# Attention with a gated MLP on one core: the last query tile's minimum taken by an accumulating tensor_scalar

## The chip, the cores and the metric

The kernel runs on one core of one Trainium2 chip. The metric is the device time of one execution in microseconds (us); of several executions the median is given.

## The reference

Block-causal attention over 8 batches x 8 heads with 576 positions of 64 dimensions, then a gated MLP over the 4608 tokens:

```python
scores = scale * np.matmul(q, k.transpose(0, 1, 3, 2))        # (8, 8, 576, 576)
mask = pos[:, None] // 64 >= pos[None, :] // 64
scores = np.where(mask, scores, -1e9)
attn = np.exp(scores - np.max(scores, axis=-1, keepdims=True))
attn = attn / (np.sum(attn, axis=-1, keepdims=True) + 1e-09)
x = np.matmul(attn, v)                                        # as (4608, 512)
h = x @ w_in                                                  # (4608, 2048)
g = h * erf(softplus(h))
return g @ w_out                                              # (4608, 512)
```

## The kernel before

The 64 heads go through attention one after the other, as a software pipeline over `n`, lines 515 to 556. In turn `n` the loop merges several lists of steps into one order: the loads of head n+3 (`load_qk`), the row maxima of head n+2 (`maxes`), the probabilities of head n (`probs`), the products with v of a pair of earlier heads (`pv`), and, after each four heads, the division by the sums (`normalise`). `merged` spreads each list evenly over the turn. Steps of the MLP for the first 6 of 16 chunks of d_ff (`moe1`, `moe_unit`, `gate`) fill the gaps of TensorE. After the last head the rest of these steps runs, and then the other 10 chunks for all tokens (lines 569 to 611).

The instructions that this order emits are put on the engines' queues by a scheduler: it goes by the emitted order, in which some kinds of steps are moved by a fixed number of instructions (`PRIO`, line 493: `pv` 74 ahead, weights 400 back or 300 ahead), and by when it takes operands and buffers to be ready. Each engine then runs its queue strictly in that order, and waits on semaphores where an operand comes from elsewhere.

The change is in `maxes(n)`. It computes the scores with queries on partitions (`mm`, L324: TensorE, into a bank of PSUM) and takes each row's maximum, negated, on VectorE (`red`, L327: a `tensor_reduce` with max and negate). The result is a column of `mx`, a [128, 6] tile in SBUF, one column for each of the five query tiles. The last query tile has 64 rows and 576 keys, more than a bank of PSUM holds, so its keys go in two halves of 288: step `d(0)` writes column 4, step `d(1)` column 5. Step `e` then takes the smaller of the two negated maxima with a one-column `tensor_tensor` (L352), transposes the first five columns on TensorE (L354, into `mt`), copies them on ScalarE (L356) and sends them by a DMA (L357) into the row of `qh` that `probs` uses two turns later.

Other lines that matter below. L312 and L313 are subtractions on GpSimd (POOL) for a head's load, L137 is GpSimd's subtraction in `gate`. L382 is VectorE's subtraction of the float16 part of the probabilities, L130 and L135 are VectorE's steps of `gate`, L469 its multiplication in `normalise`, L292 and L276 its work on v in `prep_v`. L370 and L371 are the score matmuls of `probs`; L414 and L437 are `pv`.

`bank` hands out PSUM: four buffers of one bank each in `ps_a` once the MLP runs beside attention. A score bank is free again when its reduction on VectorE has ended.

Of the kernel before, what the change touches and what calls it, by code (L numbers as in the profile page):

```python
# [15 lines left out]
AX = mybir.AxisListType  # L16
# the top word of the float64 2**-126, read as a float32
LEAST = 0.25 * (1 + 0.125) * 2.0**-13
PSUM = bass.MemoryType.PSUM

# erf(softplus(h)) as a function of r0 = tanh(T0 * h + T1).  Each step makes the next r:
#   ("S", i):    (p[0] * r_i + p[1]) ** 2
#   ("M", i, j): (r_i + p[0]) * r_j
#   ("A", i, j): p[0] * r_i + r_j
# and the value is the last r plus FIN.
PROG = [('S', 0), ('S', 1), ('M', 2, 2), ('M', 1, 3), ('M', 4, 4)]
# [8 lines left out]
def tile_attention_moe(ctx: ExitStack, tc: tile.TileContext, qk, v, w, maskrows, sels, out):  # L35
# [7 lines left out]
    F1 = 6  # L43
# [45 lines left out]
    def load_weight(whi, wlo, stage, f):  # L89
        """the two float32r parts of chunk f of both weights, out of the words of their float64"""  # L90
        for s in range(2):
            nm = f"{f}_{s}"
            raw = stage[0][0].tile([P, stage[0][2]], I32, tag=stage[0][1][s], bufs=stage[0][3], name=f"raw{nm}")[:, : 2 * DM].rearrange("p (n t) -> p n t", t=2)
            nc.sync.dma_start(raw.rearrange("p n t -> p (n t)"), w[f, s].bitcast(I32))
            top, low = raw[:, :, 1], raw[:, :, 0]
            # sign, exponent and 20 bits of mantissa as a float32 (0 for what is below its range)
            bits = stage[1][0].tile([P, stage[1][2]], I32, tag=stage[1][1], bufs=stage[1][3], name=f"bits{nm}")[:, :DM]
            nc.vector.tensor_scalar(out=bits, in0=top, scalar1=3, scalar2=0x3FFFFFF8, op0=ALU.logical_shift_left, op1=ALU.bitwise_and)  # L98
            nc.vector.scalar_tensor_tensor(out=bits, in0=top, scalar=-0x40000000, in1=bits, op0=ALU.bitwise_and, op1=ALU.bitwise_or)  # L99
            sq = stage[2][0].tile([P, stage[2][2]], F32, tag=stage[2][1], bufs=stage[2][3], name=f"sq{nm}")[:, :DM]  # L100
            nc.scalar.activation(sq, f32(top), AF.Square)
            nc.vector.scalar_tensor_tensor(out=sq, in0=sq, scalar=LEAST * LEAST, in1=f32(bits), op0=ALU.is_ge, op1=ALU.mult)  # L102
            # the low word, of the weight that the exponent gives it
            nc.vector.tensor_scalar(out=bits, in0=sq.bitcast(I32), scalar1=-0x800000, scalar2=None, op0=ALU.bitwise_and)  # L104
            nc.vector.scalar_tensor_tensor(out=f32(bits), in0=low.bitcast(U32), scalar=2.0**-52, in1=f32(bits), op0=ALU.mult, op1=ALU.mult)  # L105
            nc.scalar.copy(whi[:, s, :], sq)
            nc.gpsimd.tensor_tensor(out=sq, in0=sq, in1=f32(whi[:, s, :]), op=ALU.subtract)
            nc.gpsimd.tensor_tensor(out=wlo[:, s, :], in0=sq, in1=f32(bits), op=ALU.add)
        return whi, wlo
# [3 lines left out]
    def gate(h, name, gpool):  # L113
        """g = h * erf(softplus(h)) as a sum of two float32r parts"""
        n = h.shape[1]
        last = {}
        for k, o in enumerate(PROG):
            for i in o[1:]:
                last[i] = k
        gh, gl = (gpool.tile([P, n], F32R, tag=t, name=f"{name}_{t}") for t in ("gh", "gl"))  # L120
        regs = [mpool.tile([P, n], F32, tag="r0", name=f"{name}_r0")]
        free = [f32(gl), mpool.tile([P, n], F32, tag="r1", name=f"{name}_r1")]
        nc.scalar.activation(regs[0], h, AF.Tanh, bias=const(p1), scale=p0)  # L123
        for k, (o, pp) in enumerate(zip(PROG, pars)):
            free += [regs[i] for i in sorted(set(o[1:])) if last[i] == k]
            r = free.pop()
            if o[0] == "S":
                nc.scalar.activation(r, regs[o[1]], AF.Square, bias=const(pp[1]), scale=pp[0])  # L128
            elif o[0] == "M":
                nc.vector.scalar_tensor_tensor(out=r, in0=regs[o[1]], scalar=pp[0], in1=regs[o[2]], op0=ALU.add, op1=ALU.mult)  # L130
            else:
                nc.vector.scalar_tensor_tensor(out=r, in0=regs[o[1]], scalar=pp[0], in1=regs[o[2]], op0=ALU.mult, op1=ALU.add)
            regs.append(r)
        g = regs[-1]
        nc.vector.scalar_tensor_tensor(out=g, in0=g, scalar=fin, in1=h, op0=ALU.add, op1=ALU.mult)  # L135
        nc.scalar.copy(gh, g)  # L136
        nc.gpsimd.tensor_tensor(out=gl, in0=g, in1=f32(gh), op=ALU.subtract)  # L137
        return gh, gl
# [4 lines left out]
    def moe_unit(ws, xh, xl, o, tw, nu, u, name, first, last, spread):  # L143
        """nu chunks of d_ff over tw tokens: the steps to their g, and those to their part of o"""
        turns.append(u)
# [25 lines left out]
    def merged(*lists):  # L171
        """the steps of all lists, each list (steps, from, to) spread evenly over its part of the whole"""
        order = []
        for n, (steps, lo, hi) in enumerate(lists):
            order += [(lo + (hi - lo) * (i + 0.5) / len(steps), n, i) for i in range(len(steps))]
        return [lists[n][0][i] for _, n, i in sorted(order)]
# [4 lines left out]

# [1 line left out]
    def load_x(pool, t, tw):  # L183
# [33 lines left out]
    def moe1(ready, lag):  # L217
        """the next step of the first F1 chunks, if there is one: a unit up to its g together with an earlier unit from g on"""
        t = len(xs1)
# [19 lines left out]
    with tc.tile_pool(name="apool", bufs=2) as apool, tc.tile_pool(name="spool", bufs=1) as spool, \  # L239
# [4 lines left out]
        nc.sync.dma_start(sel, sels)  # L244
        # columns of the keys' tiles 0, 3, 4 and 1, 2 in the two parts of a head's probabilities
        p32s = [spool.tile([P, n], F32, name=f"p32_{i}") for i, n in enumerate(PN)]
# [10 lines left out]
        def bank(name):  # L257
            """a bank of PSUM; all of them take part as long as the other chunks of d_ff need none"""
            turn.append(0)
            k = len(turn) % 8 if not xs1 else 0  # L260
            if k in (2, 5):
                return ps_h.tile([P, 512], F32, tag="h", name=name)
            if k in (3,):
                return ps_o.tile([P, 512], F32, tag="o", name=name)
            return ps_a.tile([P, 512], F32, tag="a", name=name)
# [6 lines left out]
        def prep_v(b, qd, v32):  # L272
            """two float16 parts of v over its largest magnitude, and that magnitude"""
            nm = f"{b}_{qd}"
# [21 lines left out]
        def part(n, i):  # L296
            """part i of head n: kl over kh, qh over ql, kh over 5 rows that mask, qh over 5 rows that mask"""
            return qks[n % NB][:, i * S : (i + 1) * S]
# [18 lines left out]
        def maxes(n):  # L317
            """the steps to the rows' maxima, negated, in the row of t that goes with the ones"""
            mx, K = mxs[n % 2], D + 4
# [26 lines left out]
            def d(j):  # L346
                s = bank(f"s4_{n}_{j}")
                mm(s, 4, 288 * j, 288)
                red(4 + j, s[:64, :288], 64)

            def e():
                nc.vector.tensor_tensor(out=mx[:64, 4:5], in0=mx[:64, 4:5], in1=mx[:64, 5:6], op=ALU.min)  # L352
                pt = bank(f"mt{n}")
# [7 lines left out]
        def probs(n, out):  # L361
            """the steps to exp(0.125 * s - its maximum), keys on partitions, in two float16 parts"""
            K = D + 5
# [25 lines left out]
        def pv(qd, pp, prs, V, usb, rs):  # L389
            """the steps to the unnormalised outputs of heads 2pp and 2pp+1 of the quad, and to their sums"""  # L390
            vsb, vh, vl = V
            st = {}

            def ranges(q0, q1):
                """keys' tiles that a part of the queries attends to: the queries, and where their probabilities are"""
                for j in range(5):
# [21 lines left out]

            # the sums of two heads' first 384 and last 192 queries, in a group of 32 columns each
            order = []  # L420
# [24 lines left out]
        def normalise(b, qd, usbs, rs):  # L445
            nm = f"{b}_{qd}"
            # pair, tile of the sums, part of the queries, head
            ri = apool.tile([P, 2, 3, 2, 2], F32, tag="ri", name=f"ri{nm}")
# [36 lines left out]
        def late(kind, steps):  # L485
            """steps whose instructions the scheduler holds behind the next ones of the order, or ahead of some (offsets in instructions)"""
            def run(f):
# [69 lines left out]

# [1 line left out]
    N2 = 2  # L559
# [89 lines left out]
```

## Time and profile before

| | |
|---|---|
| median of 3 runs | 1399.85 us |
| the three runs | 1399.85, 1400.71, 1387.88 us |
| profiled execution | span 1407.0 us; its own time is not among the three |
| TensorE (PE) busy | 1273.8 us, 91% |
| VectorE (DVE) busy | 1013.9 us, 72% |
| ScalarE (ACT) busy | 793.2 us, 56% |
| GpSimd (POOL) busy | 602.1 us, 43% |

The profile is of one execution. PE are matmuls, PEld the loads of weights into TensorE, which overlap them. A share over the whole span mixes stages: attention with a part of the MLP fills about the first 735 us, the rest of the first six chunks and the preparation of weights the time to about 942 us, and the other chunks the end. An engine's idle time is put down to what ended it. In a line of a view that lists instructions, `mx<-s` means that the instruction writes the tile `mx` and reads the tile `s`, and `64x1 f32<-64x288 f32` gives partitions x elements of both.

### The profile page before, as it was taken

What the parts mean: (1) busy time and instruction counts of PE and PEld (TensorE: products, weight loads), DVE (VectorE), ACT (ScalarE), POOL (GpSimd) and SP (SyncE); (2) the same over time, 40 slices, a digit from 0 to 9 for tenths busy, and PEclk for the clock granted to TensorE, in tenths of its full rate; (3) what the DMA queues carried; (4) which work ended last, traced back from release to release, by engine and by line L of the source; (5) the groups of instructions that cost most, each with busy time, mean ns of one, the idle gap of its engine ahead of it and who ended that gap; (6) DMA issues with size and microseconds to landing.
All of it is one profiled execution on the core that took longest, in us unless ns stands there. A gap on an engine that the chain in (4) does not pass through costs nothing. (4 is left out here: it accounts for less than half of the span.)

```text
span 1407.0 us, 21952 instructions
## 1 busy us (share of the span) xinstructions
PE 1273.8 (91%) x8198; PEld 1026.1 (73%) x8198; DVE 1013.9 (72%) x1525; ACT 793.2 (56%) x1493; POOL 602.1 (43%) x454
## 2 busy tenths in 40 slices
PE   3798789989899898999889898779999999999998
PEld 1455567777777787777777787568888888888887
DVE  5768997788878788788697648996555555564654
ACT  1456566667666676667567455544444454445453
POOL 3757665445554554544445424562222222222221
PEclk9879899999999999999999899899999999999999
DMA  8557655757657576566623542302211311321110
GB/s 228 135 125 204 173 156 137 185 154 193 179 129 207 146 196 175 152 161 177 174 81 137 188 164 95 130 0 78 102 60 68 113 60 60 108 72 61 60 61 30
DMA packets 89370, 179.95 MB, mean 128 GB/s; under 512 B 8540, under 2 KB 27292, under 8 KB 89264
## 3 DMA queue, kind: packets, MB, share of 16 engines
q1 hardware_dynamic: 79280, 159.41, 38.1%
q0 software_dynamic: 9344, 18.97, 6.1%
q8 instruction: 65, 1.06, 0.3%
q10 hardware_dynamic: 640, 0.17, 0.1%
q14 instruction: 41, 0.34, 0.1%
HBM read 112.29 MB, written 37.75 MB: 107 GB/s over the span
## 5 line engine op out<-in xcount | busy, mean ns | idle before, releaser
L130 DVE SCALAR_TENSOR_TENSOR m_r<-m_r 128x512 f32<-128x512 f32 x288 | 232.9, 809 | 229.3 <-ACT m_r L128 225.8
L137 POOL TENSOR_TENSOR m_gl<-m_r,m_gh 128x512 fp32r<-128x512 f32 x144 | 195.5, 1357 | 443.7 <-ACT m_gh L136 359.2
L136 ACT CAST m_gh<-m_r 128x512 fp32r<-128x512 f32 x144 | 89.2, 619 | 251.9 <-DVE m_r L135 251.7
L154 PE MATMUL m_h<-xh,whi 128*128 128x256 f32 (+1 forms) x648 | 213.3, 329 | 17.3 <-DVE m_r L135 17.3
L128 ACT ACTIVATE m_r<-m_r,c 128x512 f32<-128x512 f32 x288 | 207.9, 722 | 11.0 <-ACT m_r L128 0.4
L154 PE MATMUL m_h<-xl,whi 128*128 128x256 f32 (+1 forms) x648 | 211.1, 326 | 0.3 <-DMA xl<-x_d 0.3
L154 PE MATMUL m_h<-xh,wlo 128*128 128x256 f32 (+1 forms) x648 | 211.1, 326 | 0.0
L327 DVE TENSOR_REDUCE mx<-s 64x1 f32<-64x288 f32 (+4 forms) x384 | 167.9, 468 | 56.4 <-PE s L324 53.9
L375 ACT ACTIVATE p<-t 128x288 f32<-128x288 f32 (+4 forms) x384 | 143.1, 388 | 97.9 <-PE t L371 76.2
L164 PE MATMUL o<-whi,m_gh 128*128 128x512 f32 x432 | 173.8, 403 | 6.7 <-ACT ob L209 4.3
L164 PE MATMUL o<-wlo,m_gh 128*128 128x512 f32 x432 | 173.8, 402 | 0.0
L382 DVE TENSOR_TENSOR pl<-p,ph 128x832 f16<-128x832 f32 (+1 forms) x128 | 158.5, 1240 | 18.0 <-ACT ph L381 17.8
L312 POOL TENSOR_TENSOR qk<-st,qk 64x576 fp32r<-64x576 f32 x64 | 103.2, 1613 | 157.5 <-PE s L324 55.9
L154 PEld LDWEIGHTS m_h<-xh,whi 128*128 128x128 f32 x648 | 126.6, 195 | 37.8 <-DVE m_r L135 21.9
L164 PE MATMUL o<-whi,m_gl 128*128 128x512 f32 x432 | 153.0, 402 | 0.2 <-POOL m_gl L137 0.2
L370 PE MATMUL t<-qk 69*128 69x288 f32 (+4 forms) x384 | 136.0, 355 | 12.6 <-DVE mx L327 7.0
L324 PE MATMUL s<-qk 68*128 68x256 f32 (+3 forms) x384 | 126.6, 362 | 14.3 <-DVE mx L327 8.7
L313 POOL TENSOR_TENSOR qk<-st,qk 64x576 fp32r<-64x576 f32 x64 | 111.3, 1739 | 65.5 <-DMA qk<-qk 61.7
L154 PEld LDWEIGHTS m_h<-xl,whi 128*128 128x128 f32 x648 | 126.5, 195 | 15.8 <-DMA xl<-x_d 0.6
L154 PEld LDWEIGHTS m_h<-xh,wlo 128*128 128x128 f32 x648 | 126.9, 196 | 9.4
L371 PE MATMUL t<-qk 128*128 128x288 f32 (+4 forms) x384 | 129.8, 339 | 0.0
L123 ACT ACTIVATE m_r<-m_h,c 128x512 f32<-128x512 f32 x144 | 98.8, 686 | 50.5 <-PE m_h L154 48.7
(84 smaller groups left out, 2499.1 us busy)
## 6 DMA issues: line engine op xcount, KB each, us to landing
st<-qk SPq DMA_DIRECT2D x64, 288.0 KB
qk<-qk POOLq DMA_DIRECT2D x64, 288.0 KB, 4.6
qk<-qk SPq DMA_DIRECT2D x64, 288.0 KB
x_d<-xs SPq DMA_DIRECT2D x32, 576.0 KB
raw<-w SPq DMA_DIRECT2D x32, 512.0 KB
v<-v SPq DMA_DIRECT2D x16, 640.0 KB
qk<-qk SPq DMA_DIRECT2D x64, 144.0 KB
xh<-x_d SPq DMA_DIRECT2D x18, 512.0 KB
```

The lines of the kernel that those rows point to most:

```text
L128: nc.scalar.activation(r, regs[o[1]], AF.Square, bias=const(pp[1]), scale=pp[0])
L130: nc.vector.scalar_tensor_tensor(out=r, in0=regs[o[1]], scalar=pp[0], in1=regs[o[2]], op0=ALU.add, op1=ALU.mult)
L137: nc.gpsimd.tensor_tensor(out=gl, in0=g, in1=f32(gh), op=ALU.subtract)
L154: nc.tensor.matmul(h[:, k, :], lhsT=a[:, 0, sl], rhs=x[:, cc, :], start=cc == 0 and i == 0, stop=cc == NCC - 1 and i == 2)
L164: nc.tensor.matmul(o[c], lhsT=a[:, sl], rhs=b_[:, 1, :], start=first and k == 0 and not lo and b_ is whi, stop=last and k == nu - 1 and lo)
L313: nc.gpsimd.tensor_tensor(out=t[D:, 1, :], in0=st[D:, :], in1=f32(t[D:, 1, :]), op=ALU.subtract)
L324: nc.tensor.matmul(dst[:r, :w_], lhsT=qh[:K, i * P : i * P + r], rhs=kh[:K, k0 : k0 + w_], start=True, stop=True)
L327: nc.vector.tensor_reduce(out=mx[:r, col : col + 1], in_=src, axis=AX.X, op=ALU.max, negate=True)
L370: nc.tensor.matmul(s[:kk, :w_], lhsT=kh[:K, ks], rhs=qh[:K, q0 : q0 + w_], start=True, stop=False)
L371: nc.tensor.matmul(s[:kk, :w_], lhsT=klh[:, ks], rhs=qhl[:, q0 : q0 + w_], start=False, stop=True)
L375: nc.scalar.activation(p32s[part][:kk, c : c + w_ - skip], s[:kk, skip:w_], AF.Exp, scale=SCALE)
L382: nc.vector.tensor_tensor(out=pl, in0=p, in1=ph, op=ALU.subtract)
```

## The change

Step `d(0)` now writes its negated maximum to column 5. Step `d(1)` is no reduction any more but a `tensor_scalar` on VectorE over the second half of the scores: it multiplies each score by -1, takes the minimum with the row's value in column 5 (read as one scalar for each partition), writes that back over the scores in PSUM, and gives the minimum over the row as an accumulated output to column 4. The `tensor_tensor` of step `e` is gone. The change also drops comments, which moves no line.

```diff
             def d(j):
                 s = bank(f"s4_{n}_{j}")
                 mm(s, 4, 288 * j, 288)
-                red(4 + j, s[:64, :288], 64)
+                if j == 0:
+                    red(5, s[:64, :288], 64)
+                else:
+
+                    nc.vector.tensor_scalar(out=s[:64, :288], in0=s[:64, :288], scalar1=-1.0, scalar2=mx[:64, 5:6], op0=ALU.mult, op1=ALU.min,
+                                            accum_out=mx[:64, 4:5])
 
             def e():
-                nc.vector.tensor_tensor(out=mx[:64, 4:5], in0=mx[:64, 4:5], in1=mx[:64, 5:6], op=ALU.min)
                 pt = bank(f"mt{n}")
                 nc.tensor.transpose(out=pt[:5, :P], in_=mx[:, :5], identity=ident)
```

## The prediction

> **What bounds the kernel now.** I read the shares first, then the chain that ended last, then the stages, then who waits for whom.
>
> ```profile
> PE 1273.8 (91%) x8198; PEld 1026.1 (73%) x8198; DVE 1013.9 (72%) x1525; ACT 793.2 (56%) x1493; POOL 602.1 (43%) x454
> PE 33%; DVE 6%; issue 2%; ACT 1%; POOL 0%; DVEq 0%; POOLq 0%; ACTq 0%
> 831.29 4.48 issue
> ```
>
> The second line is the chain by engine. Its shares add up to 42% of the span, because the chain, followed back from the end, is lost at 831 us (third line, its first piece). So it says nothing of the attention stage, where the changed instructions lie. For that stage the busy times by stretch have to do:
>
> ```profile
> 100.00:735.00 635.00, 572.69 (x4791) 461.58 (x4790) 524.83 (x842) 423.88 (x891) 336.78 (x246) 0.95 0.62 165
> 831.00:942.00 111.00, 87.07 (x409) 70.43 (x407) 97.53 (x114) 54.55 (x88) 55.09 (x37) 0.88 0.25 86
> 942.00:1407.00 465.00, 459.97 (x2028) 380.73 (x2028) 261.35 (x375) 222.47 (x335) 112.21 (x86) 1.00 0.21 71
> ```
>
> The columns are the stretch, its length, then the busy time of PE, PEld, DVE, ACT and POOL. In attention PE is busy 572.7 of 635.0 us (90%) and idle 62.3; DVE is busy 524.8 (83%) and idle 110.2. Neither is saturated: the two engines wait for each other. The last stretch is TensorE's alone (99%), and nothing there is touched. What attention saves therefore arrives at the end unless the stretch from 831 us, which is VectorE's (88%), takes it back; that stretch is work after the last head and starts earlier when attention ends earlier.
>
> What are the 62.3 us of PE made of? The waits of TensorE in this stretch, and the largest ones of the whole span:
>
> ```profile
> PE mt L354 <- DVE mx L352: 25.6, 22, 2.8
> PE vb L284 <- DVE vs L282: 8.1, 5, 2.8
> PE t L370 <- DVE mx L327: 6.4, 9, 1.8
> PE s L324 <- DVE mx L327: 6.4, 4, 2.3
> ...
> PE mt L354 <- DVE mx L352: 26.4, 23, 2.8
> DVE mx L327 <- PE s L324: 53.9, 82, 2.9
> ```
>
> (Engine and line, what it waited for: us in total, times, longest.) The largest single wait of TensorE in attention is the transposition of the maxima waiting for the one-column minimum: 25.6 of 62.3 us, 26.4 over the whole span. Everything behind the transposition in TensorE's queue waits with it. In the other direction DVE waits 53.9 us for the score matmuls.
>
> **Why the minimum is late.** Grouped by shape:
>
> ```profile
> L327 DVE TENSOR_REDUCE mx<-s 64x1 f32<-64x288 f32 x128 | 54.5, 440 | 15.1 <-PE s L324 13.8
> L352 DVE TENSOR_TENSOR mx<-mx 64x1 f32<-64x1 f32 x64 | 35.0, 547 | 0.2
> ...
> L352 DVE TENSOR_TENSOR mx<-mx x64: 141/148/1371, 29.8 to 730.7; 64x1 f32<-64x1 f32 x64
> ```
>
> The last line has minimum, median and maximum in ns. One column costs 0.148 us in the median, but 0.547 in the mean: 64 x 0.547 = 35.0 us where 64 x 0.148 = 9.5 would do. The other 25.5 us are held time. One head shows with whom:
>
> ```profile
> 166.58 0.80 DVE L327 TENSOR_REDUCE mx<-s 64x1 f32<-64x288 f32 x2
> 167.31 1.02 DVE L382 TENSOR_TENSOR pl<-p,ph 128x832 f16<-128x832 f32 x1
> 168.25 1.36 DVE L352 TENSOR_TENSOR mx<-mx 64x1 f32<-64x1 f32 x1
> ...
> 167.55 2.05 POOL L313 TENSOR_TENSOR qk<-st,qk 64x576 fp32r<-64x576 f32 x1 [1.44 <-DMA qk<-qk]
> ...
> 168.28 0.28 PE L154 MATMUL m_h<-xl,whi 128*128 128x256 f32 x1
> 169.76 0.27 PE L354 MATMUL mt<-ident,mx 128*5 128x128 f32 x1 [1.19 <-DVE mx L352]
> ```
>
> Both reductions of the last tile were done at 167.38. L382 stood before the minimum in DVE's queue, to 168.33; the minimum then took until 169.61, just when GpSimd's L313 ended (167.55 + 2.05 = 169.60). TensorE had nothing else from 168.56 and stood for 1.19 us. So the wait has two parts: the minimum's place in the queue, behind other DVE work, and the hold by a running GpSimd subtraction.
>
> [...]
>
> **The change part by part.**
>
> *The minimum goes.* DVE loses 64 instructions, 35.0 us of busy time.
>
> *The second reduction becomes the tensor_scalar.* No row of before shows this operation, a write to PSUM by DVE, or an accumulated output, so each term gets bounds:
>
> ```profile
> L469 DVE TENSOR_TENSOR xs<-usb,rb 128x384 f32<-128x384 f32 x32 | 17.6, 550 | 13.0 <-issue 9.2 <-PE rb L467 1.4 <-POOL qk L313 1.2
> L469 DVE TENSOR_TENSOR xs<-usb,rb 128x192 f32<-128x192 f32 x32 | 11.1, 347 | 4.3 <-PE rb L467 4.3
> L105 DVE SCALAR_TENSOR_TENSOR bits<-raw,bits 128x512 f32<-128x512 uint32 x32 | 38.7, 1210 | 0.1
> L286 DVE COPY vsb<-vb 128x2 f32<-128x2 f32 x16 | 2.5, 155 | 7.1 <-PE vb L284 7.0
> ...
> L292 DVE SCALAR_TENSOR_TENSOR vl<-v,vsb,vh x16: 1533/1550/2707, 19.7 to 690.9; 128x1280 f16<-128x1280 f32 x16
> L276 DVE TENSOR_REDUCE vm<-v x16: 1464/1468/1486, 9.9 to 654.9; 128x1 f32<-128x1280 f32 x16
> ...
> 511.92 0.83 DVE L327 TENSOR_REDUCE mx<-s 64x1 f32<-64x288 f32 x2
> 512.79 0.15 DVE L352 TENSOR_TENSOR mx<-mx 64x1 f32<-64x1 f32 x1
> ```
>
> - The stream: L469 reads PSUM and writes a column for each column. From 192 to 384 columns it grows by (550 - 347)/192 = 1.06 ns a column, so 288 columns are 347 + 96 x 1.06 = 449 ns against the reduction's 440: +0.01 us. The upper end is the slowest stream of the rows, L105 with 1210/512 = 2.36 ns a column, 680 ns: +0.24. I take 0.01, L469 being the nearest; a loss below the reduction's time is excluded, since all streams over float32 in these rows need more than 1 ns a column.
> - The scalar for each partition: L292 has one, L276 none, both over 1280 columns: 1550 - 1468 = 82 ns. Ends 0 and 0.08; I take 0.08.
> - The accumulated value to column 4: nothing if it comes with the stream, 0.155 us (L286) if it is an instruction of its own; I take 0.14. [...]
> - The added wait, for column 5: two reductions in a row overlap by 0.07 us (2 x 0.45 in 0.83), while the dependent minimum starts 0.04 us after the second. Where the tensor_scalar follows `d(0)`'s reduction directly it loses that 0.11 us. Behind it stands all later DVE work, and TensorE's next use of the bank. Ends 0 and 0.11; I take 0.11.
>
> Together +0.34 us a head, 64 x 0.34 = 21.8 us; the ends are 64 x 0.01 = 0.6 and 64 x (0.24 + 0.08 + 0.155 + 0.11) = 37.4. Against 35.0 removed, DVE's busy time changes by -13.2 (ends -34.4 and +2.4). Part of the 25.5 held us comes back, where the next DVE instruction also meets the running GpSimd one; between nothing and all of it, I take half, 12.7. So DVE is about even: -0.5 us.
>
> *The transposition's operand is earlier.* Column 4 is now written in `d(1)`'s place in DVE's queue, not behind L382 and others. In the head above it would be there at about 167.38 + 0.34 = 167.72, with TensorE arriving at 168.56: the 1.19 us are gone. The longest wait is of the other kind, and goes too:
>
> ```profile
> 469.24 2.71 DVE L292 SCALAR_TENSOR_TENSOR vl<-v,vsb,vh 128x1280 f16<-128x1280 f32 x1
> 471.88 1.01 DVE L382 TENSOR_TENSOR pl<-p,ph 128x832 f16<-128x832 f32 x1
> 472.81 0.14 DVE L352 TENSOR_TENSOR mx<-mx 64x1 f32<-64x1 f32 x1
> ...
> 473.01 0.28 PE L354 MATMUL mt<-ident,mx 128*5 128x128 f32 x1 [2.78 <-DVE mx L352]
> ...
> 513.54 0.28 PE L354 MATMUL mt<-ident,mx 128*5 128x128 f32 x1
> ```
>
> At 512 us, one of the heads with least room, the pair of reductions ends at 512.75 and the transposition starts, unstalled, at 513.54: 0.79 us, more than the 0.34 that the new instruction adds, and more than the 0.57 of the upper ends. With TensorE's order as it is, all 26.4 us of this wait go.
>
> *What is late next.* TensorE then reaches its other gates on DVE 26.4/64 = 0.4 us a head earlier, while DVE's own work is as long as before. If TensorE set the pace alone, 26.4 us would be saved; if DVE did, its -0.5. DVE's 110.2 idle us, a large part of which it spends waiting for these very score matmuls, speak for TensorE; the 6.4 + 6.4 + 8.1 us of other waits on DVE for the opposite. I take half: **-13 us, 1399.85 - 13 = 1387**. The profile's span is 7 us above the median of the runs; the difference is carried over to the median.
>
> Moved besides: only column numbers (4 and 5 swap), and no DMA. `e`'s copy and DMA (L356, L357) come earlier by what the transposition gains, two turns ahead of their use, where nothing waits for it.
>
> **The rivals.**
>
> *The gain comes back.* DVE's queue is as long as before, and TensorE stands at the next bank that DVE has not emptied. For it: DVE at 83%, and a bank that is held 0.34 us longer. Against it: DVE's idle time. Time: 1399.85 - 0.5, with what is left between -6 and +5: 1394 to 1405. [...]
>
> *Slower: the transposition moves up.* The scheduler may now place L354 directly behind the second score matmul, since no minimum stands between. TensorE would then stand, in every head, for the whole tensor_scalar: 0.44 + 0.34 = 0.78 us, 64 x 0.78 = 50 us, in place of 26.4: 1399.85 + 23.5 = 1423; with half the heads moved, 1411. It decides where less than 0.78 us of TensorE's work is left between the two. For it: the scheduler's order follows its own idea of when operands are ready, and now that is earlier. Against it: step `e` still stands a sixth of a turn behind `d(1)`, and TensorE has much other work.
>
> *Another order.* One instruction less is emitted for each head, and `PRIO` counts in instructions (74 of them for `pv`), so orders shift a little on all queues: 10 to 15 us either way, without any tie to the steps above. The three runs of before themselves spread by 12.8 us.
>
> *It doesn't do what it says:* if a one-column instruction for the accumulator remains and is held by GpSimd as L352 was, the 25.5 us stay on DVE, but in `d(1)`'s place, and half of TensorE's wait with them: 1399.85 - 13 + 13 = 1400, as in the first rival.
>
> **How the numbers follow.** About 1%, 14 us, is what a measurement of this kernel can tell from no change. Forecast case (8 to 26 us saved) 0.55, of it 0.38 beyond 1% and 0.17 within. Gain comes back, in either form, 0.22: 0.20 within, 0.02 faster. Transposition moves up 0.13: 0.12 slower, 0.01 within. Another order 0.10: 0.03, 0.04, 0.03. Faster 0.43, same 0.42, slower 0.15. The range starts at the full saving with the lower end of DVE's costs, 1399.85 - 26.4 - 2 = 1371, and ends where half the transpositions have moved, 1411. The likeliest case alone is 1373 to 1392.
>
> **What would show it.** Right: L352 and its wait are gone, waits of L354 on DVE below 5 us, PE idle between 100 and 735 us near 45 instead of 62; the new instruction near 0.53 us with about 0.14 beside it. Wrong: L354 waiting for the new line in most heads (moved up); waits of L324, L370 or L414 on DVE grown by about 20 us (came back); the new instruction above 0.68 us; L130 or L382 longer by the full 25 us.

## The result: 1.1% slower

| | before | after |
|---|---|---|
| median of 14 runs each | 1400.66 us (1387.88 to 1411.43) | 1413.97 us (1402.43 to 1420.94) |
| ratio, 95% interval | 1 | 1.0111 (1.0083 to 1.0140) |
| profiled execution: span | 1407.0 us | 1418.7 us (its own time 1420.94) |

The forecast was 1387 us, 1371 to 1411. The time came out on the other side, above the range. All ratios and clocks here are estimates without the executions that took over 1.5% longer than the fastest of their kernel, so 1.0111 is not the quotient of the two medians, 1.0095; this takes four of 12 from `old_ops_new_order`, whose medians with all of them give 1.0082, and at most two from any other kernel.

The lines of the profile after that answer to those of before: shares and chain by engine, the same three stretches (length, then busy PE, PEld, DVE, ACT, POOL, then the granted clock of TensorE, DMA share, GB/s), the granted clock in 40 slices, and TensorE's wait for the new line.

```profile
PE 1289.4 (91%) x8198; PEld 1038.5 (73%) x8198; DVE 1003.1 (71%) x1525; ACT 790.3 (56%) x1493; POOL 593.9 (42%) x454
...
PEclk9798799999998889998999999789999999999999
...
PE 58%; DVE 16%; DMA 4%; issue 3%; ACT 1%; POOL 0%; ACTq 0%; SPq 0%; DVEq 0%; POOLq 0%
```

```profile
100.00:735.00 635.00, 576.45 (x4694) 463.88 (x4697) 493.33 (x816) 411.57 (x880) 326.88 (x242) 0.91 0.61 163
831.00:942.00 111.00, 89.16 (x443) 73.14 (x443) 92.53 (x111) 55.77 (x89) 51.22 (x34) 0.89 0.27 91
942.00:1407.00 465.00, 461.94 (x2026) 381.83 (x2026) 269.34 (x383) 225.39 (x340) 117.25 (x89) 0.99 0.20 68
```

```profile
PE mt L358 <- DVE s L353: 18.6, 12, 3.7
```

TensorE's busy time in attention is the trap. TensorE is busy longer than before, 576.5 us against 572.7, and idle less, 58.6 against 62.3. But it got less done: 4694 matmuls against 4791. The column that goes with this is the clock, 0.91 against 0.95. A matmul at half clock takes longer and counts as busy: in the trace of after, the 128x256 matmuls of L154 took 282 ns in the median between 415.2 and 428.6 us (clock 1.00) and 415 ns between 428.8 and 442.2 us (clock 0.50). Over the two stretches 80 matmuls took 13.26 us against 116 in 11.44 us, in rows shown further down. So the sum of TensorE's waits doesn't show the loss; whether single waits brought the clock down is asked below. This execution is the slowest of the 14, and a second profile of the same program, also below, is much nearer to before. The transposition (L354, now L358) waits less in sum, 18.6 us against 26.4, in 12 places against 23, but its longest wait grew from 2.8 to 3.7 us.

The new instruction by itself is what was worked out:

```profile
L353 DVE TENSOR_SCALAR_CACHE_REDUCE s<-s,mx x64: 428/511/519, 29.7 to 723.3; 64x288 f32<-64x288 f32 x64
L353 DVE DVE_READ_ACCUMULATOR s<-s,mx x64: 129/132/135, 30.1 to 723.8; 64x1 f32 x64
```

(Minimum, median, maximum in ns.) 0.511 + 0.132 us, in two instructions, never held: the largest value is 8 ns above the median, where the one-column minimum went up to 1.371 us.

### The profile page after: what moved, and what is told of

It is laid out like the page before. It is cut to its first block, busy times and chain, and to the rows that moved or that the text cites. A ratio compares the mean times of both kernels' runs of the same rounds, so it can differ in the third digit from the quotient of the medians.

```text
span 1418.7 us, 22016 instructions
## 1 busy us (share of the span) xinstructions
PE 1289.4 (91%) x8198; PEld 1038.5 (73%) x8198; DVE 1003.1 (71%) x1525; ACT 790.3 (56%) x1493; POOL 593.9 (42%) x454
## 4 chain that ended last, share of the span: by engine, by line
PE 58%; DVE 16%; DMA 4%; issue 3%; ACT 1%; POOL 0%; ACTq 0%; SPq 0%; DVEq 0%; POOLq 0%
PE m_h L154 22%; PE o L164 22%; DVE m_r L130 6%; DMA v<-v 3%; PE u L418 3%; PE s L324 2%; PE t L375 2%; PE t L374 2%; DVE pl L386 2%; DVE sq L102 1%; PE rt L457 1%; DVE bits L105 1%; PE rb L471 1%; DVE vl L292 1%; DVE bits L99 1%
## 5 line engine op out<-in xcount | busy, mean ns | idle before, releaser
L130 DVE SCALAR_TENSOR_TENSOR m_r<-m_r 128x512 f32<-128x512 f32 x288 | 236.9, 823 | 229.0 <-ACT m_r L128 225.6
L137 POOL TENSOR_TENSOR m_gl<-m_r,m_gh 128x512 fp32r<-128x512 f32 x144 | 198.4, 1378 | 452.6 <-ACT m_gh L136 439.1
L154 PE MATMUL m_h<-xh,whi 128*128 128x256 f32 (+1 forms) x648 | 214.8, 332 | 25.1 <-DVE m_r L135 19.9
L154 PE MATMUL m_h<-xh,wlo 128*128 128x256 f32 (+1 forms) x648 | 214.2, 331 | 0.0
L128 ACT ACTIVATE m_r<-m_r,c 128x512 f32<-128x512 f32 x288 | 207.9, 722 | 11.1
L154 PE MATMUL m_h<-xl,whi 128*128 128x256 f32 (+1 forms) x648 | 213.3, 329 | 0.8 <-DMA xl<-x_d 0.8
L327 DVE TENSOR_REDUCE mx<-s 128x1 f32<-128x128 f32 (+4 forms) x320 | 141.8, 475 | 56.3 <-PE s L324 53.8
L312 POOL TENSOR_TENSOR qk<-st,qk 64x576 fp32r<-64x576 f32 x64 | 99.3, 1552 | 161.1 <-PE t L375 36.8
L386 DVE TENSOR_TENSOR pl<-p,ph 128x832 f16<-128x832 f32 (+1 forms) x128 | 152.9, 1195 | 19.3 <-ACT ph L385 18.9
L154 PEld LDWEIGHTS m_h<-xh,whi 128*128 128x128 f32 x648 | 128.4, 198 | 47.8 <-DVE m_r L135 26.6
L374 PE MATMUL t<-qk 69*128 69x288 f32 (+4 forms) x384 | 138.6, 361 | 10.8 <-DVE mx L327 5.2
L154 PEld LDWEIGHTS m_h<-xl,whi 128*128 128x128 f32 x648 | 128.3, 198 | 16.8 <-DMA xl<-x_d 1.1
L324 PE MATMUL s<-qk 68*128 68x256 f32 (+3 forms) x384 | 128.4, 367 | 9.6 <-ACT p L379 3.9
L154 PEld LDWEIGHTS m_h<-xh,wlo 128*128 128x128 f32 x648 | 128.3, 198 | 10.4 <-issue 0.6
L375 PE MATMUL t<-qk 128*128 128x288 f32 (+4 forms) x384 | 134.0, 350 | 0.0
L313 POOL TENSOR_TENSOR qk<-st,qk 64x576 fp32r<-64x576 f32 x64 | 107.1, 1673 | 52.7 <-DMA qk<-qk 50.5
```

The costliest lines, as they stand in the source:

```text
L154: nc.tensor.matmul(h[:, k, :], lhsT=a[:, 0, sl], rhs=x[:, cc, :], start=cc == 0 and i == 0, stop=cc == NCC - 1 and i == 2)
L313: nc.gpsimd.tensor_tensor(out=t[D:, 1, :], in0=st[D:, :], in1=f32(t[D:, 1, :]), op=ALU.subtract)
L324: nc.tensor.matmul(dst[:r, :w_], lhsT=qh[:K, i * P : i * P + r], rhs=kh[:K, k0 : k0 + w_], start=True, stop=True)
L327: nc.vector.tensor_reduce(out=mx[:r, col : col + 1], in_=src, axis=AX.X, op=ALU.max, negate=True)
L374: nc.tensor.matmul(s[:kk, :w_], lhsT=kh[:K, ks], rhs=qh[:K, q0 : q0 + w_], start=True, stop=False)
L375: nc.tensor.matmul(s[:kk, :w_], lhsT=klh[:, ks], rhs=qhl[:, q0 : q0 + w_], start=False, stop=True)
```

## The experiments

Each measured figure is the ratio to the kernel before in the same series, with its 95% interval. "Clock" is the mean granted clock of TensorE over the executions that the ratio is taken from; the kernel before has 0.954 to 0.957 in these series, and the change itself has 0.946. That clock and time go together shows within the 14 executions of the changed kernel, one program in one order: 0.955 at 1402.43 us, 0.939 at 1420.23 us, 11 us for 0.01.

### Order or instructions?

The edit changes two things: the instructions, and the order that the scheduler gives to every queue. Each was tried alone. A queue's order is pinned by dependencies of the class NoSync between neighbours:

```diff
+    for a, b in zip(places, places[1:]):   # for each engine, the emitted instructions in the order of its queue
+        tc.add_manual_dep(made[b], made[a].name, ...)
```

`new_ops_old_order`: the changed kernel, its queues in the order of before.

> The changed kernel, with every engine's queue held in the order that the kernel before has (the minimum left out of it; in heads 1, 3 and 4, whose two halves stood the other way round, the tensor_scalar is put behind the reduction). Theory A, the loss is in the new order that the edit makes the scheduler write: in the old order the new instructions are no loss, time 0.985 to 0.998 of before, TensorE's wait at the transposition below 5 us, half-clock time of TensorE not above the 141 us of before. Theory B, the loss is in the accumulating instruction itself: 1.005 to 1.015 again.

Measured: 1.0036 (0.9999 to 1.0073), clock 0.948, between the ranges of the two theories.

`old_ops_new_order`: the kernel before, its queues in the order of after, the minimum right behind the second reduction.

> The kernel before, with every queue held in the order of the changed kernel; the one-column minimum stands directly behind the second reduction. Theory A: 1.005 to 1.02 of before, with half-clock time near the 173 us of the changed kernel. Theory B: 0.99 to 1.00, since the accumulating instruction isn't there.

Measured: 1.0065 (1.0026 to 1.0103), clock 0.952. 0.36% and 0.65% add up to about the 1.1% of both. So a loss needs none of the new instructions: the order, with the old minimum in it, makes one that is clear of zero. That it is the larger part rests on the two middle values, since the intervals overlap. The other part, 0.36%, has an interval that touches zero.

In the old order the transposition behaves as predicted. The first two fences are of `new_ops_old_order`, the attention stretch and a wait of TensorE; the third is the group in the page of before that goes with the second:

```profile
100.00:735.00 635.00, 587.42 (x4894) 476.75 (x4894) 514.13 (x847) 428.01 (x908) 340.73 (x250) 0.94 0.63 168
```

```profile
PE t L374 <- DVE mx L327: 11.8, 17, 1.8
```

```profile
L370 PE MATMUL t<-qk 69*128 69x288 f32 (+4 forms) x384 | 136.0, 355 | 12.6 <-DVE mx L327 7.0
```

TensorE's wait for L353 has no line left, and its idle time in attention is 635.0 - 587.4 = 47.6 us instead of 62.3. Part of the gain is back at the next gate, where the first score matmul of `probs` waits until a reduction (L327) has freed a bank (11.8 us against 7.0). And the runs are not faster, at a lower clock.

### The minimum's hold, and the minimum itself

In the trace of before, 30 of the 64 minima took 0.24 to 1.37 us, and each of these ended 10 to 19 ns after an instruction of GpSimd (L312, L313, L137, L107 or L108); the other 34 took 0.14 to 0.16 us. The `tensor_scalar` of one element (L281) in the same trace took 131 to 142 ns all 16 times, 12 of them with GpSimd busy for more than half of that. `no_hold_old_order` keeps the minimum, in before's order, but as a `tensor_scalar` with one tensor and one scalar for each partition:

```diff
-                nc.vector.tensor_tensor(out=mx[:64, 4:5], in0=mx[:64, 4:5], in1=mx[:64, 5:6], op=ALU.min)
+                nc.vector.tensor_scalar(out=mx[:64, 4:5], in0=mx[:64, 4:5], scalar1=mx[:64, 5:6], scalar2=None, op0=ALU.min)
```

> The kernel before in its own order, only the minimum is a tensor_scalar whose second operand is one scalar for each partition in place of a second tensor: the same place in all queues, but not held by GpSimd, 0.15 us each time. Prices the hold alone. If the hold was what TensorE waited for: the 26.4 us of waits at the transposition fall by some 15, time 0.988 to 0.996. If the wait only moves to the next DVE instruction and TensorE's next gate: 0.998 to 1.002. No theory expects it slower.

Measured: 1.0006 (0.9973 to 1.0038), clock 0.951. In its trace the wait behind the minimum is down from 26.4 to 11.1 us, and VectorE is busy 998.8 us in all instead of 1013.9, 15.1 us less. (The 64 minima of before take 25.5 us more than 64 times their median.) `no_min_old_order` leaves that line out: the last tile's maximum is that of its first half alone.

> The kernel before in its own order with the minimum left out and both halves reduced as before, so the last tile's maximum is that of the first half alone. It is the removal without the accumulating instruction. Theory A: like the new instructions in the old order, or faster by what the 0.2 us of the longer instruction cost, 0.98 to 0.995. Theory B: 0.98 to 0.99, and clearly faster than the new instructions in the old order.

Measured: 0.9996 (0.9966 to 1.0025), clock 0.950. With the queues as they were, all 35 us of the minimum on VectorE and the whole 26.4 us wait behind it are worth nothing that can be measured, by the interval at most 0.34%. That is the case against the forecast's premise: this wait was not what attention paid for.

`no_min_new_order` leaves the same line out and lets the scheduler choose its order. The transposition then depends on the first half alone.

> The kernel before without the minimum (both halves reduced, the last tile's maximum is that of the first half alone), the scheduler free. It has neither the one-column minimum nor the accumulating instruction, and its written order finishes 31 of the 54 MLP units within attention, where before finishes 37 and the changed kernel 34. Theory A2, the loss is the MLP units that the new order leaves behind attention, some 5 us each: 1.015 to 1.025. Theory B, the accumulating instruction costs: 0.99 to 1.00.

Measured: 0.9935 (0.9903 to 0.9967), clock 0.955: the only kernel whose whole interval lies below 1, and not a complete one. `new_ops_and_min` adds the minimum in this form to the changed kernel, free order:

```diff
             def e():
+                nc.vector.tensor_scalar(out=mx[:64, 4:5], in0=mx[:64, 4:5], scalar1=mx[:64, 5:6], scalar2=None, op0=ALU.min)
```

> The changed kernel with a one-column minimum (one tensor and one scalar for each partition, so not held by GpSimd) put back ahead of the transposition, where it does nothing to the value; the scheduler free. It has all of the change's instructions and one more, and its written order finishes 38.8 MLP units within attention. Theory A2: 0.988 to 0.998, faster than before by the 1.8 units more. Theory B: 1.01 to 1.02.

Measured: 1.0040 (1.0009 to 1.0071), clock 0.950. One more instruction a head, and faster than the 1.0111 without it; against a second series of the change (1.0088, 1.0061 to 1.0115, see below) the intervals overlap. With the scheduler free the order differs too, and that the order makes the difference is likely but not shown by this run.

### How much of the MLP is left behind attention

Counted by the matmuls into h up to the last matmul of `pv`, the new order has 34 of the MLP's units within attention where the old has 37; the expectations below take this count for the cause. `new_ops_max_later` moves the maxima's steps in the order of emission (29.5 units), `before_3_units_held` holds three units back in the kernel before:

```diff
-        PRIO = {"pv": -74, "w1": 400, "w2": -300}
+        PRIO = {"pv": -74, "w1": 400, "w2": -300, "max": 40}
```

```diff
+    for i in held:     # the matmuls into h of units 34 and up
+        tc.add_manual_dep(i, last.name, ...)   # behind the last matmul of pv
```

> The changed kernel, its instructions unaltered, with the steps of the row maxima moved back by 40 instructions in the emitted order; the scheduler free. Its written order finishes 29.5 MLP units within attention. Theory A2: 1.02 to 1.04 of before, slower than the changed kernel. Theory B: 1.00 to 1.015, as the changed kernel.

> The kernel before, unaltered but for one thing: TensorE's matmuls of MLP units 34 and up stand behind attention's last products with v, so that 34 units are finished within attention as in the changed kernel, and not 37. All queues are the same up to the end of attention (TensorE's first 7149 of 10566 places). Theory A2, if it is the number of units alone: 1.006 to 1.013. If it takes the thinner filling all along attention, with TensorE's clock lower there: 1.000 to 1.005, since here only the last heads lose theirs.

Measured: 1.0053 (1.0022 to 1.0083) and 1.0037 (1.0009 to 1.0065). The theory falls. `new_ops_max_later`, with fewer units than the change, is not slower than it. Holding three units costs something, but `new_ops_and_min` with 38.8 units is slower than before, and `no_min_new_order` with 31 is the fastest. The count does not order the kernels.

### The clock

Each kernel in its own order, with useless matmuls into the transposition's bank ahead of the transpositions that waited over 0.6 us: 67 in 11 heads of after, 90 in 20 heads of before.

```diff
+                for _ in range(FILL.get(n, 0)):
+                    nc.tensor.matmul(pt, lhsT=ident16, rhs=ident16[:, None, :].broadcast_to([P, 4, P]), start=True, stop=True)
                 nc.tensor.transpose(out=pt[:5, :P], in_=mx[:, :5], identity=ident)
```

> The changed kernel in its own order, with 67 matmuls of no use (float16, 128x512, into the bank of the transposition) put on TensorE directly ahead of the transposition in the eleven heads in which it waited over 0.6 us in the profile; they fill some 85% of each wait and have no other reader. Theory C, long waits of TensorE drop its granted clock to half for several windows after them, and this is the second half of the loss: the mean granted clock rises from 0.946 to 0.951 or more and the time falls to 1.000 to 1.007 of before (from 1.011). If the clock doesn't follow these waits: 1.010 to 1.016, since the extra matmuls can only add.

> The kernel before in its own order, with 90 such matmuls ahead of the transposition in the 20 heads in which it waited over 0.6 us. Theory C: the waits here are shorter (2.8 us at most), so less is to be gained: 0.992 to 1.000. If the clock doesn't follow these waits: 1.000 to 1.006.

Measured: after 1.0043 (1.0008 to 1.0078) at clock 0.952 instead of 0.946; before 0.9991 (0.9961 to 1.0021) at 0.960 instead of 0.954. Work that computes nothing, put where TensorE stood, takes away more than half of the loss against the 14 runs of the change, which are another series; against its second series (1.0088) it is half, with intervals that overlap. From before it takes nothing measurable although its clock rises as much, so the rise alone does not settle the time. That the filling also costs time where it outlasts a wait is a likely reason, which no run shows.

Second profiles of both:

> The kernel before once more, for a second profile. Theory D, the profile on which the prediction was made is of an unusually slow execution: span 1390 to 1400 us here, TensorE idle 8 us or more below the 128.8 us of that profile. If that profile is typical: TensorE idle 126 to 131 us, span near 1400 or above.

> The changed kernel once more, for a second profile: 34 MLP units within attention by its order, half-clock time 150 to 180 us, TensorE idle 122 to 129 us.

Single times 1398.13 and 1404.32 us, clocks 0.958 and 0.952. TensorE is idle 129.8 us in the second profile of before and was idle 133.2 us in the first, so the first was not unusual. After's second execution is one of its faster ones; its half clock, 2 x 0.048 x 1402.1 = 135 us, is below the 150 to 180 expected. The attention stretch of both, and of a third profile of the change (`after_same_chip`, 1414.08 us, near the median of the change):

```profile
100.00:735.00 635.00, 577.88 (x4853) 467.73 (x4853) 520.91 (x837) 427.72 (x900) 340.25 (x247) 0.95 0.63 167
100.00:735.00 635.00, 580.30 (x4872) 464.19 (x4871) 513.51 (x839) 425.50 (x908) 337.17 (x247) 0.94 0.62 166
100.00:735.00 635.00, 574.23 (x4768) 461.61 (x4769) 498.69 (x825) 417.81 (x894) 331.55 (x244) 0.92 0.61 165
```

One program in one order has 4694, 4768 and 4872 matmuls in this stretch, at 0.91, 0.92 and 0.94. Single traces of two kernels may therefore differ by as much without any difference between the kernels, and what an edit is worth is read from its 5 to 14 executions.

### Where the long waits come from

The trace of after, in order of time (start, duration, and in brackets the idle time of the engine before it with what ended it):

```profile
425.89 1.49 DVE L276 TENSOR_REDUCE vm<-v 128x1 f32<-128x1280 f32 x1 [2.90 <-DMA v<-v]
...
427.30 1.01 DVE L386 TENSOR_TENSOR pl<-p,ph 128x832 f16<-128x832 f32 x1
...
428.23 0.51 DVE L353 TENSOR_SCALAR_CACHE_REDUCE s<-s,mx 64x288 f32<-64x288 f32 x1
...
428.94 0.37 PE L358 MATMUL mt<-ident,mx 128*5 128x128 f32 x1 [2.31 <-DVE s L353]
```

VectorE stands 2.90 us for the load of v, with L386 and the new instruction queued behind L276; TensorE then stands 2.31 us. In the trace of after such a place comes five times: the transpositions at 265.7, 345.4, 428.9, 475.2 and 654.0 us wait 1.64, 2.76, 2.31, 2.19 and 3.72 us. The stretches of 13.5 us behind these five (PE's busy time is the first column behind the length, the clock the third from the end), and as the third row one ahead of a wait:

```profile
265.70:279.20 13.50, 12.69 (x101) 10.49 (x102) 10.49 (x18) 8.45 (x19) 9.12 (x8) 1.00 0.69 168
345.40:358.90 13.50, 13.50 (x123) 10.91 (x124) 9.95 (x17) 9.86 (x23) 6.08 (x6) 0.87 0.81 213
415.20:428.70 13.50, 11.44 (x116) 9.50 (x114) 10.61 (x19) 8.11 (x17) 4.34 (x4) 1.00 0.82 217
428.70:442.20 13.50, 13.26 (x80) 10.36 (x81) 6.80 (x13) 7.28 (x17) 5.18 (x5) 0.50 0.33 80
475.20:488.70 13.50, 13.50 (x98) 10.77 (x100) 8.06 (x16) 6.95 (x16) 6.51 (x6) 0.62 0.46 106
653.90:667.40 13.50, 13.44 (x79) 10.74 (x80) 7.19 (x14) 6.05 (x14) 4.07 (x4) 0.50 0.36 94
```

The third row is the stretch ahead of the wait shown above: clock 1.00, 116 matmuls in 11.44 us. The row under it follows the wait: clock 0.50, 80 matmuls in 13.26 us, with VectorE busy 6.80 us instead of 10.61 and the transfers at 80 GB/s instead of 217. The granted clock is either 1.00 or 0.50 all through the traces of before and after. So, by twice the missing clock times 13.5 us, the five stretches behind waits hold 0 + 3.5 + 13.5 + 10.3 + 13.5 = 41 us at half clock. The four longest waits of the transposition in before (1.82, 2.78, 1.89 and 1.79 us) have this behind them:

```profile
215.90:229.40 13.50, 13.15 (x120) 10.03 (x120) 11.33 (x17) 8.75 (x20) 4.04 (x4) 0.87 0.48 118
473.00:486.50 13.50, 11.82 (x85) 9.51 (x87) 9.74 (x15) 7.17 (x15) 5.11 (x5) 0.87 0.53 133
570.50:584.00 13.50, 13.48 (x125) 10.67 (x126) 8.25 (x16) 9.69 (x22) 6.81 (x6) 0.87 0.49 120
705.60:719.10 13.50, 12.12 (x122) 9.49 (x123) 12.60 (x21) 9.43 (x21) 5.75 (x5) 1.00 0.32 77
```

That is 10.5 us at half clock, a quarter of after's. Over all of attention, twice the missing clock times 635 us gives 114 us for after and 64 us for before: some 30 of the 50 us between them lie behind these waits. In the second profile of the change the same five transpositions wait 1.2 to 2.7 us, and the 13.5 us behind them have clocks of 0.87, 0.87, 0.87, 0.50 and 1.00, some 24 us at half clock. So the waits come back in another execution, and their price varies. VectorE stood for the load of v in before too, but less (first line, the group in before). And in `no_min_new_order`, the fastest kernel, it stood as long as in after (second line). There the transposition needs only the reduction of the first half, and it waited for it twice, 3.6 us in all. The two lines:

```profile
L276 DVE TENSOR_REDUCE vm<-v 128x1 f32<-128x1280 f32 x16 | 23.6, 1475 | 18.9 <-DMA v<-v 18.9
```

```profile
DVE vm L276 <- DMA v<-v: 29.0, 12, 10.6
```

The first try at this was to issue 12 of the 16 loads of v five transfers earlier, each kernel otherwise in its order, beside a plain run of the change on the same chip (one of the 12 places, as the queue's entries and not as code):

```diff
-    SyncE:  ..., x_d, qk, st, xh, xl, v, ...
+    SyncE:  ..., v, x_d, qk, st, xh, xl, ...
```

> The changed kernel in its own order on every queue, but with the loads of v of the last 12 quads issued five transfers earlier on SyncE (some 10 us). In the changed kernel VectorE stands 28.7 us in front of the maximum of v (L276), 17.1 us of it in the heads whose transposition then waits 1.6 to 3.7 us. Theory V (these five long waits, by the clock that falls behind them, are most of what the new order costs): the wait at L276 falls below 14 us, 10 of them at the start, no transposition of the maxima waits over 2 us, the half clock in the profile comes down by 20 us or more, and the ratio falls to 1.003 to 1.007. Rival (the long waits only move to other places, or the order costs its time elsewhere): L276 no longer waits, but other waits of over 2 us take the place, and the ratio stays at 1.008 to 1.013.

> The changed kernel once more, as the measure of the run beside it: a ratio of 1.008 to 1.014 by what was measured before. If the chip matters more than the kernel it falls outside.

> The kernel before in its own order, with the same 12 loads of v five transfers earlier. There VectorE stands 18.9 us in front of L276, 9.9 of it at the start, and only one transposition behind such a wait stands over 1.5 us. Theory V: little to win, 0.996 to 1.000. Rival (the earlier load delays the loads of q and k that it is moved past): 1.001 to 1.005.

> The changed kernel's instructions in the order of the kernel before, with the same 12 loads of v five transfers earlier. That order without the earlier loads measured 1.0036 (0.9999 to 1.0073). Theory V: 7.5 us of waiting at L276 (3.5 of it at one place) go, 0.998 to 1.002. Rival: unchanged, 1.002 to 1.005.

Measured: 1.0450 (1.0413 to 1.0487), 1.0088 (1.0061 to 1.0115), 1.0418 (1.0389 to 1.0446), 1.0418 (1.0371 to 1.0465). A miss, and neither theory had it. The waits of SyncE's queue, first in after, then in `after_early_v`:

```profile
SPq L269 <- DVE vl L292: 33.7, 11, 10.9
```

```profile
SPq L269 <- DVE vl L292: 125.5, 14, 14.2
```

The tile of v has one buffer, and L292, its last reader, runs 35 us after L276 in the trace of after (382.1 and 417.1 us, the next load following at 418.6). The load was already issued when that buffer came free. Moved ahead, it only blocks SyncE, with the loads of q and k behind it: TensorE's wait for them in `maxes` (L324) is 34.7 us in `after_early_v` and 1.0 us in after. So the wait was taken from its other end. L276 of the last 12 groups goes later in VectorE's queue, right behind the next `tensor_scalar` (in before: minimum) that is at least three places away; its result is not used for some 30 us (again the queue's entries, shortened):

```diff
-    VectorE:  ..., L276, L386, ..., L353, ...
+    VectorE:  ..., L386, ..., L353, L276, ...
```

> The changed kernel in its own order on every queue, but with the maximum of v (L276) of the last 12 quads placed later in VectorE's queue: right behind the next tensor_scalar (L353) that is at least three places away, 4 to 14 places later. Nothing uses L276's result for some 30 us, so the instructions that were queued behind it no longer stand still for the load of v. Theory V: the idle time of VectorE before L276 falls from 28 us to about 11 (10 of it at the start), no transposition of the maxima waits over 2 us, the half clock in the profile falls from 154 to 173 us to below 145, and the ratio falls from 1.0088 to 1.0111 to 1.002 to 1.006. Rival (the long waits move elsewhere): the transposition's waits go, the half clock and the ratio stay (over 145 us, 1.008 to 1.012).

> The kernel before in its own order with the same edit, L276 right behind the next one-column minimum (L352), 8 to 16 places later. 9 us of VectorE's waiting there go, at four places of 1.2 to 3.7 us. Theory V: 0.996 to 0.999. Rival: no difference, 0.999 to 1.002.

Measured: 1.0047 (1.0020 to 1.0074) at clock 0.950, and 1.0014 (0.9983 to 1.0045) at 0.951. In the kernel before the edit is worth nothing that can be measured, as the rival had it. In the changed kernel, moving 12 instructions of one queue takes more than half of the loss against the 14 runs of the change, where the intervals are apart, and just under half against its second series (1.0088, another chip), where they overlap a little. The instructions of L276 with what ended VectorE's idle time before them, and the attention stretch, in `after_vm_later`; then the same idle time in after:

```profile
L276 DVE TENSOR_REDUCE vm<-v x16: 1464/1472/1487, 9.9 to 638.1; 128x1 f32<-128x1280 f32 x16
...
  DMA v<-v: 9.9, 1
```

```profile
100.00:735.00 635.00, 582.77 (x4901) 463.80 (x4901) 518.83 (x844) 427.49 (x913) 350.02 (x249) 0.94 0.62 167
```

```profile
  DMA v<-v: 28.7, 11
```

VectorE's idle time before L276 is down to the one wait at the start. In attention 4901 matmuls were done instead of 4694, at 0.94 instead of 0.91; but the unaltered change has 4872 at 0.94 in its faster execution above, so this pair of traces proves little, and the 12 executions carry the result. Against what was expected two long waits of the transposition remained, 4.3 and 2.1 us. The longer one is of another kind:

```profile
372.83 2.79 DVE L130 SCALAR_TENSOR_TENSOR m_r<-m_r,m_r 128x512 f32<-128x512 f32 x1
...
375.55 2.71 DVE L292 SCALAR_TENSOR_TENSOR vl<-v,vsb,vh 128x1280 f16<-128x1280 f32 x1
...
378.18 2.22 DVE L386 TENSOR_TENSOR pl<-p,ph 128x832 f16<-128x832 f32 x1
...
380.32 0.51 DVE L353 TENSOR_SCALAR_CACHE_REDUCE s<-s,mx 64x288 f32<-64x288 f32 x1
...
381.03 0.37 PE L358 MATMUL mt<-ident,mx 128*5 128x128 f32 x1 [4.28 <-DVE s L353]
```

Three instructions in a row take about two to four times their median (0.69 us for L130, 1.55 for L292, 1.01 for L386), while GpSimd ran four instructions one after the other beside them (372.3 to 379.5 us). That they take the hold which the minimum had before is not shown: L292 took 2.71 us in a row of before, too.

None of the complete kernels is faster than the kernel before.

## Why the prediction was wrong

- **The step that failed first: "With TensorE's order as it is, all 26.4 us of this wait go."** The sentence is right and its condition was not met. With the order pinned, the wait is gone and TensorE's idle time is 47.6 us, near the 45 that was named. In the order that the scheduler chose, "Column 4 is now written in `d(1)`'s place in DVE's queue, not behind L382 and others" did not hold: in 17 of the 64 heads the new instruction stood directly behind L386, the former L382 (with the order pinned in 2), in five of them behind L276's wait for v as well, and 18.6 us remained, in fewer and longer pieces.
- **The step that failed second: "I take half: -13 us".** Even with the order pinned the time is 1.0036, not 0.991, and leaving the minimum out altogether gives 0.9996. The half weighed two idle times against each other; neither is a price. The sum was made in idle microseconds of TensorE at full clock, while the granted clock stood in the quoted rows of before (0.95 in attention) and was not used. For `new_ops_old_order` the traces show 14.7 us less idle time in attention, and the runs a clock of 0.948 against 0.957; at the 11 us for 0.01 above, that would take back some 10 us. This is an estimate, from one trace of each kernel, and what is left of the difference up to +0.36% stays open.
- **The rival with the right name, "Another order", got 0.10** and 10 to 15 us either way "without any tie to the steps above". Its size was right by luck, as it came from no mechanism. And it had a tie: the same wait, on the same engine, set up by a load that the sum did not look at. The 18.9 us that VectorE stands before L276 were a row of before. How much of the loss runs through this is not settled: the two edits that go at it (filling the waits, moving L276) each take about half.
- **VectorE's terms held.** Predicted 0.53 + 0.14 us, measured 0.51 + 0.13. No run of the kernel before shows the 0.14 us for the accumulated value as an instruction of its own, which was the author's estimate; the trace of after has one, `DVE_READ_ACCUMULATOR`, 64 times with 0.132 us in the median. VectorE's busy time changed by 1003.1 - 1013.9 = -10.8 us where -0.5 was taken and -34.4 to +2.4 bounded. Gone are 35.0 us; the new pair costs 64 x (0.511 + 0.132) = 41.2 us where 64 reductions took 64 x 0.440 = 28.2; so 35.0 - 13.0 - 10.8 = 11.2 us came back elsewhere, close to the 12.7 put down for the hold. Most of the difference to -0.5 is the wait for column 5 (7 us priced), which no duration shows. None of it decided the time. (The upper ends of the new instruction's terms add up to 0.585 us, where the prediction once has 0.57; nothing hangs on it.)
- **"The transposition moves up" did not happen:** 12 waits, not 64, though its 1411 to 1423 us hold the measured time, by luck. "The gain comes back" is what the pinned order shows (11.8 us against 7.0 at L374), but not what made the time.

## What to carry to other kernels

In a kernel whose order a scheduler makes, one instruction less can be a new order of everything: before pricing a wait, pin the old order and see what the edit is worth there, and look at what stands in front of the moved instruction in its queue. Read the granted clock beside TensorE's busy time: here waits with a smaller sum, but longer ones among them, went with a lower clock and a longer time. An instruction that waits for a transfer while its result is not needed for 30 us belongs behind the urgent ones in the queue, and moving its load instead cost 4% here, because the buffer was the limit.

## What the hardware showed

In the trace of after a wait of TensorE of 2.2 to 2.3 us was followed by 10 to 13.5 us at half clock, though TensorE was then busy 98 to 100% of the time (rows at 428.7 and 475.2); waits of 1.6 and 2.8 us in the same trace by none and by 3.5 us.

Whether the clock falls goes with how a wait lies. In the traces of before and after, all changes of the granted clock (47 and 45 of them, between 1.00 and 0.50) lie multiples of 3.41 us apart. Of the nine waits whose following stretch is shown above, the seven that have 1.79 us or more within one such step were followed by half clock. The two that have no more than 0.87 us (265.7, in after) and 1.43 us (705.6, in before) within one were not. From 33 us on, where the record of the clock begins, 11 steps at full clock in before and 17 in after had TensorE busy less than 46% of the time, and none of them was followed by another at full clock. A step with 46.4% was (before, 940.8 us). The clock also fell behind busier steps, of up to 87% (before, 360.5 us) and 86% (after, 534.5 us), so the share does not settle it alone.

What differs between the traces of after and before is how long half clock lasts. In attention (100 to 735 us) the clock fell 14 times in after and 15 times in before, for 116 and 65 us in all. The runs do not show what sets this length: the wait at 428.9 us in after, 2.31 us, had 13.5 us of half clock behind it, and the wait at the same place in `after_again`, 2.36 us at 426.7 us, had 3.4.
